# Splitting the first slice of a weight load in two transfers, and the order of the matmuls that read it

## The chip, the core and the metric

The kernel runs on one core of a Trainium2 chip. The metric is the device time of one execution in microseconds (us), given as the median of several executions. Engines are named as in the profile: PE is the matrix engine (PEld its weight loads), DVE the vector engine, ACT the scalar engine, POOL the GpSimd engine, SP the engine that here only issues DMAs.

## What is computed

The program is a retention layer (linear attention with a decay for each head) followed by a two-layer feed-forward block. The reference, cut to what matters:

```python
# q, k, v: (4 batches, 8 heads, 768 steps, 64), float32
gamma = 1.0 - 2.0 ** (-5.0 - np.arange(H)); scale = 1.0 / np.sqrt(D)
for t in range(S):
    state = gamma[None, :, None, None] * state + einsum('bhd,bhe->bhde', k[:, :, t], v[:, :, t])
    y[:, :, t] = scale * einsum('bhd,bhde->bhe', q[:, :, t], state)
x = y.transpose(0, 2, 1, 3).reshape(B * S, H * D)     # 3072 tokens x 512
h = x @ w_in                                          # w_in: 512 x 2048
g = h * np.cos(h)
out = g @ w_out                                       # w_out: 2048 x 512
```

## The kernel before, in words

The order of all work is written out by hand (a manual schedule); each engine runs its own instructions in the order in which the program emits them, and semaphores make an instruction wait for what it reads or overwrites. A small model of time (`Clock`) and a list of PSUM banks (`Banks`, seven banks of 128x512 float32) decide only which bank a unit of work takes next: the one that the model thinks comes free first.

**Retention.** The 768 steps are cut into 6 chunks of 128. A *pair* p (there are 12) is one chunk of two batches. For each pair, q, k and v are loaded (256 KB each; `load`, L130), scaled by the decays and turned to bf16 (`conv_q` L179, `conv_v` L186, `conv_k` L192, on DVE, ACT or POOL), q and k are transposed (by PE in `stage_t`, L214, copied out by DVE at L198; for later pairs by DMA, L224), the 128x128 scores are formed (`stage_a`, L241) and masked by DVE (`stage_m`, L250), and `half_y` (L263 and L268) sums the two terms of y in PSUM, which ACT copies into `xt` (L272). `xt[g]` holds the transposed tokens of a *group* g of two pairs: 4 blocks of 128 model rows (index i, `KIN` = 4) by 512 tokens, of which the first 256 are of the group's first pair and the last 256 of its second. `stage_s` (L285, L290) moves the state on.

**Feed-forward.** An *F unit* is 128 of the 2048 hidden columns for the 512 tokens of one group: four matmuls, one for each i, that sum into one bank (`unit_f`, L316), then cos on ACT (L305) and the product on DVE into `gt` (L309). `pair_f(p, r)` (L327) does the same for one pair's 256 tokens and the four hidden blocks f = 4r to 4r+3, two of them to a bank, so sixteen matmuls of 256 columns into two banks. An *O unit* (`unit_o`, L340) is four matmuls of the second layer; four parts make one block of 128 tokens, copied out by ACT (L347) and stored by SP (L348).

**Weights.** `w_in` is loaded as four slices of 512 hidden columns, one transfer each (`load_w_in`, L135; 512 KB in bf16, read as float32 and cast on the way), `w_out` as four slices of 512 rows (`load_w_out`, L140). F blocks 0 to 3 read slice 0, blocks 4 to 7 slice 1, and so on. All of these are issued by POOL, in one queue with most loads of q, k and v, and with POOL's own conversions between them. The stretch that matters, in POOL's order: v of pair 0, v of pair 1, w_in slices 0 and 1, conversions of v (half of pair 0's first batch at L386, then three whole ones at L186), w_in slice 2, slice 3, w_out slices 0 to 2, k and q of pair 2, w_out slice 3, and v of pair 2, then pair 3.

**The order on PE around the change.** Pairs 0 and 1 go through the retention stages, with filler matmuls (`warm`, L374) between them; then

```python
    half_y(1, 1)
    stage_s(1, nc.scalar.copy)
    pair_f(0, 0)
    pair_f(1, 0)
    for f in range(4, 16):
        unit_f(0, f)
```

so the first four F blocks of group 0 are done pair by pair, and the other twelve as whole units. After them come the O units of group 0 with pair 2's stages between them (`stage_t(2, ...)` after the eighth O unit).

Of the kernel before, what the change touches and what calls it, by code (L numbers as in the profile page):

```python
# [11 lines left out]
BF16 = mybir.dt.bfloat16  # L12
# [35 lines left out]
def kernel(  # L48
# [9 lines left out]
    nc = tc.nc  # L58
# [3 lines left out]
    DM = H * D  # L62
    DF = moe_w_in.shape[1]
    HP = H // 2
    KIN = DM // 128
# [15 lines left out]
    def sb(shape, dt, name):  # L81
        return const.tile(shape, dt, name=name)

    clk = Clock()
    banks = Banks([psum.tile([128, 512], FP32, name=f"bank{i}") for i in range(7)], clk)
# [6 lines left out]
    lnsc = sb([128, 1], FP32, "lnsc")  # L92
    lgv = sb([128, H], FP32, "lgv")

    w_in_sb = [sb([128, KIN, 512], BF16, f"w_in{r}") for r in range(4)]
    w_out_sb = sb([128, KOUT, DM], BF16, "w_out_sb")


# [11 lines left out]
    xt = [sb([128, KIN, 4 * C], BF16, f"xt{i}") for i in range(2)]  # L110
    gt = [sb([128, KOUT, 4 * C], BF16, f"gt{i}") for i in range(2)]
# [13 lines left out]
    def load(eng, p, names):  # L125
        bp, c = divmod(p, NC)
        for n in names:
            t, src = SRC[n[0]]
            b = int(n[1])
            eng.dma_start(  # L130
                out=t[SLOT[p]][b],
                in_=src[2 * bp + b, :, ds(c * C, C)].rearrange("h t d -> t h d"))

    def load_w_in(r):
        nc.gpsimd.dma_start(  # L135
            out=w_in_sb[r],
            in_=moe_w_in[:, ts(r, 512)].rearrange("(i p) f -> p i f", p=128))

    def load_w_out(r):
        nc.gpsimd.dma_start(  # L140
            out=w_out_sb[:, ts(r, 4), :],
            in_=moe_w_out[ts(r, 512), :].rearrange("(p j) m -> p j m", j=4))

    def w_in_t(i, f):
        return w_in_sb[f // 4][:, i].rearrange("p (m j) -> p j m", j=4)[:, f % 4, :]


    load(nc.sync, 0, ("q0", "k0", "q1"))
# [127 lines left out]
    def stage_s(p, copy_st):  # L276
        c = p % NC
        n = p % NB
        if c == NC - 1:
            return  # L280
        for b in range(2):
            for a in range(HP):
                for j in range(2):
                    h = 2 * a + j
                    nc.tensor.matmul(  # L285
                        st_ps[ts(j, 64), b, a, :], lhsT=qk[n][:, b, 1, h, :],
                        rhs=vs[n][:, b, h, :], start=(c == 0 and b == 0 and a == 0),
                        stop=True, skip_group_check=True)
        for j in range(2):
            copy_st(out=stb[(p + 1) % 2][ts(j, 64), :, :, ts(j, 64)], in_=st_ps[ts(j, 64)])  # L290
            clk.run("act" if copy_st == nc.scalar.copy else "dve", 0.65, clk.pe + 0.3)
        clk.run("pe", 0.25)
# [9 lines left out]
    def act(bank, out):  # L302
        cb = cosb[f_no[0] % 3]
        f_no[0] += 1
        nc.scalar.activation(out=cb, in_=bank, func=AF.Sin, bias=halfpi)  # L305
        if len(out.shape) == 3:
            cb = cb.rearrange("p (f t) -> p f t", f=2)
            bank = bank.rearrange("p (f t) -> p f t", f=2)
        nc.vector.tensor_tensor(out=out, in0=bank, in1=cb, op=ALU.mult)  # L309
        clk.run("pe", 0.87)  # L310
        return clk.run("dve", 0.69, clk.run("act", 0.69, clk.pe + 0.1) + 0.1)

    def unit_f(g, f):
        bank = banks.take()
        for i in range(KIN):
            nc.tensor.matmul(bank, lhsT=w_in_t(i, f), rhs=xt[g % 2][:, i, :],  # L316
                             start=(i == 0), stop=(i == KIN - 1))
        banks.give(bank, act(bank, gt[g % 2][:, f, :]))

    def pair_f(p, r, parts=(0, 1)):  # L320

        g, hf = divmod(p, 2)
        for f in [4 * r + 2 * i for i in parts]:
            bank = banks.take()
            for e in range(2):
                for i in range(KIN):
                    nc.tensor.matmul(bank[:, ts(e, 256)], lhsT=w_in_t(i, f + e),  # L327
                                     rhs=xt[g % 2][:, i, ts(hf, 256)],
                                     start=(i == 0 and e == 0), stop=(i == KIN - 1),
                                     skip_group_check=True)  # L330
            banks.give(bank, act(bank, gt[g % 2][:, f : f + 2, ts(hf, 256)]))

    o_bank = {}

    def unit_o(g, j, part):
# [42 lines left out]
    def attend(p):  # L378
        for it in [stage_a(p, b) for b in range(2)]:
            stage_m(p, it)  # L380

    load(nc.gpsimd, 1, ("v0", "v1"))
    load_w_in(0)
    load_w_in(1)
    hh = H // 2
    nc.gpsimd.tensor_tensor(  # L386
        out=vs[0][:, 0, hh:], in0=vf[SLOT[0]][0][:, hh:, :],
        in1=gk[:, 0, hh:].unsqueeze(2).to_broadcast([128, hh, D]), op=ALU.mult)
    conv_v(0, nc.gpsimd, (1,))
    conv_v(1, nc.gpsimd)  # L390
    load_w_in(2)

    warm(8)
# [39 lines left out]
    banks.give(spare, clk.pe)  # L433
    half_y(1, 1)
    stage_s(1, nc.scalar.copy)
    pair_f(0, 0)
    pair_f(1, 0)
    for f in range(4, 16):
        unit_f(0, f)

# [76 lines left out]
    for g in range(2, NG + 1):  # L517
        for s in range(16):
            hf, r = divmod(s, 8)
            p = 2 * (g + 1) + hf  # L520
# [52 lines left out]
```

## Time and profile before

| | |
|---|---|
| median of 6 executions | 210.85 us (209.83 to 211.23) |
| the profiled execution: its time, its span | 211.23 us, 209.4 us |
| granted PE clock | 1.00 |
| busy: PE, DVE, ACT, POOL | 95%, 54%, 55%, 49% of the span |
| w_in: transfers, each, median to landing | 4, 512 KB, 9.0 us |

The span runs from the first to the last instruction of the program; the profiled execution's time is 1.8 us longer. In the views below, times are us from the start of the span, and "L327" is a line of the kernel before. "Busy" of PE counts matmuls that overlap their neighbours, so a full PE row says that PE had no gap, not that it ran at its peak. A DMA's *landing* is the moment when its semaphore tells the waiting engine that all of it has arrived; the trace gives the time from issue to landing for each line, and for a single transfer when the window is narrowed to it.

### The profile page before, as it was taken

What the parts mean: (1) busy time and instruction counts of PE and PEld (TensorE: products, weight loads), DVE (VectorE), ACT (ScalarE), POOL (GpSimd) and SP (SyncE); (2) the same over time, 40 slices, a digit from 0 to 9 for tenths busy, and PEclk for the clock granted to TensorE, in tenths of its full rate; (3) what the DMA queues carried; (4) which work ended last, traced back from release to release, by engine and by line L of the source; (5) the groups of instructions that cost most, each with busy time, mean ns of one, the idle gap of its engine ahead of it and who ended that gap; (6) DMA issues with size and microseconds to landing.
All of it is one profiled execution on the core that took longest, in us unless ns stands there. A gap on an engine that the chain in (4) does not pass through costs nothing.

```text
span 209.4 us, 4170 instructions
## 1 busy us (share of the span) xinstructions
PE 198.7 (95%) x1629; PEld 113.7 (54%) x1652; DVE 114.1 (54%) x188; ACT 114.6 (55%) x193; POOL 102.1 (49%) x118
## 2 busy tenths in 40 slices
PE   7687999999999999999999999999999999999993
PEld 3356554558897555555545455555545444444452
DVE  5691784472967472968874575565565233333000
ACT  6586784057898227477844734744544654553120
POOL 7998325569999999999999500000000000000000
PEclk9999999999999999999999999999999999999999
DMA  6999999969999999988899191181101101110222
GB/s 155 330 239 196 215 243 289 324 172 268 360 231 239 259 262 300 236 263 178 284 128 321 50 103 50 52 105 50 50 3 50 50 0 53 50 52 10 90 72 81
DMA packets 36644, 33.83 MB, mean 162 GB/s; under 512 B 26768, under 2 KB 29072, under 8 KB 36624
## 3 DMA queue, kind: packets, MB, share of 16 engines
q0 software_dynamic: 7808, 20.98, 37.0%
q1 hardware_dynamic: 28672, 12.49, 27.6%
q8 instruction: 13, 0.21, 0.5%
q10 hardware_dynamic: 144, 0.10, 0.1%
q14 instruction: 7, 0.06, 0.1%
HBM read 27.26 MB, written 6.29 MB: 160 GB/s over the span
## 4 chain that ended last, share of the span: by engine, by line
PE 89%; POOL 4%; DMA 4%; issue 1%; DVE 0%; POOLq 0%; DVEq 0%
PE bank L340 38%; PE bank L316 31%; PE bank L327 9%; DMA w_in<-in_moe_w_in_dram 4%; PE bank L241 3%; PE bank L263 2%; PE bank L268 2%; PE bank L357 2%; POOL vf L130 2%; POOL kf L130 1%; PE st_ps L285 1%; PE bank L214 1%; POOL qf L130 1%; DVE ob L362 0%; POOL rel L152 0%
## 5 line engine op out<-in xcount | busy, mean ns | idle before, releaser
L309 DVE TENSOR_TENSOR gt<-bank,cosb 128x512 bf16<-128x512 f32 x96 | 65.4, 690 | 64.4 <-ACT cosb L305 64.1
L305 ACT ACTIVATE cosb<-bank,halfpi 128x512 bf16<-128x512 f32 x96 | 65.6, 688 | 51.5 <-PE bank L316 46.4
L340 PE MATMUL bank<-w_out_sb,gt 128*128 128x512 bf16 x358 | 88.4, 379 | 0.7 <-issue 0.3
L316 PE MATMUL bank<-xt,w_in 128*128 128x512 bf16 x293 | 73.7, 380 | 1.2 <-issue 0.9
L340 PEld LDWEIGHTS <-gt 128*128 128x128 bf16 x368 | 35.5, 98 | 41.2
L316 PEld LDWEIGHTS <-w_in 128*128 128x128 bf16 x304 | 33.5, 114 | 30.1
L250 DVE TENSOR_TENSOR am<-bank,mask 128x512 bf16<-128x512 f32 x48 | 30.4, 681 | 0.8 <-PE bank L241 0.8
L130 POOL DMA_DIRECT2D vf<-in_v_dram x23 | 20.2, 884 | 5.5 <-DMA w_out_sb<-in_moe_w_out_dram 5.5
L347 ACT COPY ob<-bank 128x512 f32<-128x512 f32 x23 | 13.4, 585 | 16.9 <-PE bank L340 16.8
L130 POOL DMA_DIRECT2D kf<-in_k_dram x23 | 20.6, 896 | 3.1 <-DMA w_out_sb<-in_moe_w_out_dram 1.6
L186 POOL TENSOR_TENSOR vs<-vf,gk 128x512 bf16<-128x512 f32 x21 | 21.4, 1040 | 0.2 <-DMA vf<-in_v_dram 0.2
L179 POOL TENSOR_TENSOR qk<-qf,gq 128x512 bf16<-128x512 f32 x18 | 18.5, 1049 | 3.0 <-DMA qf<-in_q_dram 2.3
L327 PE MATMUL bank<-xt,w_in 128*128 128x256 bf16 x160 | 18.4, 273 | 1.6 <-DMA w_in<-in_moe_w_in_dram 1.6
L192 ACT CAST qk<-kf 128x512 bf16<-128x512 f32 x24 | 13.8, 613 | 10.4 <-DMA kf<-in_k_dram 10.4
L327 PEld LDWEIGHTS <-w_in 128*128 128x128 bf16 x160 | 17.2, 114 | 2.0 <-DMA w_in<-in_moe_w_in_dram 1.7
L130 POOL DMA_DIRECT2D qf<-in_q_dram x18 | 16.3, 904 | 1.7 <-DMA w_in<-in_moe_w_in_dram 1.7
L272 ACT CAST xt<-bank 128x512 bf16<-128x512 f32 x24 | 13.0, 587 | 7.3 <-PE bank L268 7.2
L268 PE MATMUL bank<-am,vs 128*64 128x128 bf16 x192 | 11.7, 220 | 0.0
L263 PEld LDWEIGHTS <-stb 128*64 128x64 bf16 x160 | 8.8, 109 | 4.3 <-issue 3.1
L290 DVE CAST stb<-st_ps 64x512 bf16<-64x512 f32 x12 | 8.2, 686 | 4.9 <-PE st_ps L285 4.7
L263 PE MATMUL bank<-qkt,stb 128*64 128x128 bf16 x160 | 10.7, 222 | 0.1
L268 PEld LDWEIGHTS <-vs 128*64 128x64 bf16 x192 | 10.0, 110 | 0.5 <-issue 0.4
(40 smaller groups left out, 77.5 us busy)
## 6 DMA issues: line engine op xcount, KB each, us to landing
kf<-in_k_dram POOLq DMA_DIRECT2D x23, 256.0 KB, 5.5
vf<-in_v_dram POOLq DMA_DIRECT2D x23, 256.0 KB, 5.5
out_dram<-ob SPq DMA_DIRECT2D x23, 256.0 KB, 2.0
qf<-in_q_dram POOLq DMA_DIRECT2D x18, 256.0 KB, 5.4
w_in<-in_moe_w_in_dram POOLq DMA_DIRECT2D x4, 512.0 KB, 9.0
w_out_sb<-in_moe_w_out_dram POOLq DMA_DIRECT2D x4, 512.0 KB, 14.0
qf<-in_q_dram SPq DMA_DIRECT2D x6, 256.0 KB, 8.3
kf<-in_k_dram SPq DMA_DIRECT2D x1, 256.0 KB, 3.4
```

Source lines behind the costliest of these rows:

```text
L130: eng.dma_start(out=t[SLOT[p]][b], in_=src[2 * bp + b, :, ds(c * C, C)].rearrange("h t d -> t h d"))
L179: eng.tensor_tensor(out=qk[p % NB][:, b, 0], in0=qf[SLOT[p]][b], in1=bc(gq, p % NC), op=ALU.mult)
L186: eng.tensor_tensor(out=vs[p % NB][:, b], in0=vf[SLOT[p]][b], in1=bc(gk, p % NC), op=ALU.mult)
L192: nc.scalar.copy(out=qk[p % NB][:, b, 1], in_=kf[SLOT[p]][b])
L250: nc.vector.tensor_tensor(out=am[p % 2][b][j], in0=ap[j], in1=mask.unsqueeze(1).to_broadcast([128, HP, 128]), op=ALU.mult)
L263: nc.tensor.matmul(yp[ts(j, 64), a, :], lhsT=stb[p % 2][:, b, a, ts(j, 64)], rhs=qt(n, b, a), start=True, stop=False, skip_group_check=True)
L268: nc.tensor.matmul(yp[ts(j, 64), a, :], lhsT=vs[n][:, b, 2 * a + j, :], rhs=am[p % 2][b][j][:, a, :], start=(c == 0), stop=True, skip_grou ...
L305: nc.scalar.activation(out=cb, in_=bank, func=AF.Sin, bias=halfpi)
L309: nc.vector.tensor_tensor(out=out, in0=bank, in1=cb, op=ALU.mult)
L316: nc.tensor.matmul(bank, lhsT=w_in_t(i, f), rhs=xt[g % 2][:, i, :], start=(i == 0), stop=(i == KIN - 1))
L327: nc.tensor.matmul(bank[:, ts(e, 256)], lhsT=w_in_t(i, f + e), rhs=xt[g % 2][:, i, ts(hf, 256)], start=(i == 0 and e == 0), stop=(i == KIN ...
L340: nc.tensor.matmul(bank, lhsT=gt[g % 2][:, f, ts(j, 128)], rhs=w_out_sb[:, f, :], start=(f == 0), stop=(f == KOUT - 1))
```

## The change

Slice 0 of w_in is now loaded by two transfers into two tiles: one holds model rows 0 to 255 (i = 0, 1), the other rows 256 to 511 (i = 2, 3). The two stand where the one stood in POOL's order. The first four F blocks are no longer done pair by pair. `first_f` takes four banks, one for each block f of 0 to 3, each holding all 512 tokens. It first runs i = 0 and 1 of the four blocks on the first pair's 256 tokens, then the same on the second pair's 256 tokens (sixteen matmuls of 256 columns in all), and then i = 2 and 3 of each block on all 512 tokens (eight matmuls of 512 columns), each block followed by its cos and product. `gt[0]` is written in whole rows of 512 tokens, as `unit_f` does.

```diff
-    w_in_sb = [sb([128, KIN, 512], BF16, f"w_in{r}") for r in range(4)]
+    w_in_sb = [sb([128, KIN, 512], BF16, f"w_in{r}") for r in range(1, 4)]
+    w_in_0 = [sb([128, KIN // 2, 512], BF16, f"w_in0_{i}") for i in range(2)]
...
     def load_w_in(r):
         nc.gpsimd.dma_start(
-            out=w_in_sb[r],
+            out=w_in_sb[r - 1],
             in_=moe_w_in[:, ts(r, 512)].rearrange("(i p) f -> p i f", p=128))
+
+    def load_w_in_0():
+        for i in range(2):
+            nc.gpsimd.dma_start(
+                out=w_in_0[i],
+                in_=moe_w_in[ts(i, DM // 2), :512].rearrange("(i p) f -> p i f", p=128))
...
     def w_in_t(i, f):
-        return w_in_sb[f // 4][:, i].rearrange("p (m j) -> p j m", j=4)[:, f % 4, :]
+        w = w_in_sb[f // 4 - 1][:, i] if f > 3 else w_in_0[i // 2][:, i % 2]
+        return w.rearrange("p (m j) -> p j m", j=4)[:, f % 4, :]
...
+    def first_f():
+        bank = [banks.take() for _ in range(4)]
+        for hf in range(2):
+            for f in range(4):
+                for i in range(2):
+                    nc.tensor.matmul(bank[f][:, ts(hf, 256)], lhsT=w_in_t(i, f),
+                                     rhs=xt[0][:, i, ts(hf, 256)],
+                                     start=(i == 0 and hf == 0), stop=False,
+                                     skip_group_check=True)
+            clk.run("pe", 0.87)
+        for f in range(4):
+            for i in range(2, KIN):
+                nc.tensor.matmul(bank[f], lhsT=w_in_t(i, f), rhs=xt[0][:, i, :],
+                                 start=False, stop=(i == KIN - 1), skip_group_check=True)
+            clk.run("pe", -0.44)
+            banks.give(bank[f], act(bank[f], gt[0][:, f, :]))
...
     load(nc.gpsimd, 1, ("v0", "v1"))
-    load_w_in(0)
+    load_w_in_0()
     load_w_in(1)
...
     stage_s(1, nc.scalar.copy)
-    pair_f(0, 0)
-    pair_f(1, 0)
+    first_f()
     for f in range(4, 16):
         unit_f(0, f)
```

## The prediction

> **What bounds the kernel now.** I read the chain of work that ended last first, in order of time (start, length, what):
>
> ```profile
> 6.25 3.49 POOL vf L130 x4
> 9.74 8.36 DMA w_in<-in_moe_w_in_dram
> 18.14 3.68 PE bank L327 x32
> 21.87 10.31 PE bank L316 x47
> 32.67 6.42 PE bank L340 x29
> 39.09 0.89 PE bank L214 x16
> 202.46 3.51 PE bank L357 x32
> ```
>
> Up to 18.1 us the end is set by one transfer, slice 0 of w_in, which lands at 9.74 + 8.36 = 18.10. From there to the end the chain is PE without a gap. So a microsecond won for PE near 18 is won at the end, provided that nothing else becomes late. The waits of PE say the same: in the whole span it waits for a DMA once.
>
> ```profile
> PE bank L327 <- DMA w_in<-in_moe_w_in_dram: 1.6, 1, 1.6
> ```
>
> Next the timeline of PE and its weight loads around that place (start, length, engine, line, count; in brackets the idle time before and what ended it):
>
> ```profile
> 15.72 0.27 PE L268 MATMUL bank<-am,vs 128*64 128x128 bf16 x2
> 16.11 0.47 PE L285 MATMUL st_ps<-vs,qk 128*64 128x64 bf16 x16
> 18.13 3.42 PEld L327 LDWEIGHTS <-w_in 128*128 128x128 bf16 x32 [1.67 <-DMA w_in<-in_moe_w_in_dram]
> 18.14 3.68 PE L327 MATMUL bank<-xt,w_in 128*128 128x256 bf16 x32 [1.56 <-DMA w_in<-in_moe_w_in_dram]
> 21.55 10.15 PEld L316 LDWEIGHTS <-w_in 128*128 128x128 bf16 x48
> 21.87 10.31 PE L316 MATMUL bank<-xt,w_in 128*128 128x512 bf16 x47
> ```
>
> PE is through with retention at 16.58. The 32 matmuls of 256 columns take 21.55 - 18.13 = 3.42 us, 0.107 each; those of 512 columns follow each other by (10.31 - 0.38)/46 = 0.216. One of the 48 is missing from the records, so the first most likely began one step before 21.87, at 21.65.
>
> Last, where the next slices land. The view of line L135, narrowed in time until one and then two issues are in it, gives
>
> ```profile
> DMA to landing us min/median/max: 8.4/8.4/8.4
> DMA to landing us min/median/max: 8.4/9.2/10.1
> ```
>
> so slice 1, issued at 10.48, lands at 20.6. Narrowed likewise to the other two, issued at 15.32 and 16.1: 7.8 and 9.6 us, that is 23.1 and 25.7. The four land 2.5, 2.5 and 2.6 us apart although the first two were issued 0.74 apart: the slices are served one after another at about 2.5 us each.
>
> **The change part by part.**
>
> *First half of slice 0.* Half the bytes of a slice served in 2.5 us: it should land 1.25 us ahead of the whole, at 16.85. PE is free at 16.58, and the first pair's `xt` is there: ACT's copies of `xt` run as
>
> ```profile
> 15.22 1.77 ACT L272 CAST xt<-bank 128x512 bf16<-128x512 f32 x3
> ```
>
> of which the first, the last of pair 0, ends near 15.8, and the last two (pair 1) by 16.99. If the matmuls on pair 0 wait for all of `xt`, they start at 17.0 instead. Sixteen matmuls of 256 columns: 1.72 us, to 18.57 (pair 1's eight start at 17.71, after 16.99). The second half lands at 18.1, before it is asked for. Eight matmuls of 512 columns: 1.73, to 20.30 (20.45 with the later start). The same columns run through PE as before, so PE's work is unchanged (16 x 0.107 + 8 x 0.216 = 3.45 against 3.42); it is only started earlier.
>
> *What is late next.* F block 4 needs slice 1, which lands at 20.6. So PE stops again at 20.3 and goes on at 20.63 (after slice 0 the wait ended 0.03 behind the landing). Gain: weight loads 21.55 - 20.63 = 0.92, matmuls 21.65 - 20.64 = 1.01. I take **1.0 us**. This gate makes the term robust: anywhere up to 20.6 - 3.45 = 17.15, a later start of the first half costs nothing. Had slice 1 come before 20.3, the gain would be the whole 1.25 to 1.35.
>
> *One more transfer on POOL's queue.* An issue on L135 (512 rows) takes 0.78 us, on L140 0.56 (fewer, longer rows); a half slice (256 rows) lies between, say 0.66, so two cost 1.32 for 0.78: 0.54 more (0.34 to 0.78). Queued behind it on POOL: slice 1, the conversions of v, slices 2 and 3, w_out, and pair 2's loads. POOL has idle time in the way:
>
> ```profile
> 9.74 1.52 POOL L135 DMA_DIRECT2D w_in<-in_moe_w_in_dram  x2
> 11.56 0.61 POOL L386 TENSOR_TENSOR vs<-vf,gk 128x256 bf16<-128x256 f32 x1 [0.30 <-ACT qk L192]
> 12.33 3.04 POOL L186 TENSOR_TENSOR vs<-vf,gk 128x512 bf16<-128x512 f32 x3 [0.15 <-DMA vf<-in_v_dram]
> 15.32 1.55 POOL L135 DMA_DIRECT2D w_in<-in_moe_w_in_dram  x2
> ```
>
> The 0.30 and 0.15 take 0.45 of the 0.54; v's last conversion ends at 15.46 instead of 15.37 (15.70 at worst). PE reads it at 15.72. And PE's later gate leaves 17.15 - 16.58 = 0.57 of slack. So this costs nothing; without POOL's idle time it would still be inside those 0.57 us. Slice 2 is issued 0.1 later (0.33 at worst) and would be needed at 20.63 + 16 x 0.216 = 24.1, against a landing at 23.1.
>
> *One more transfer on the DMA engines.* Its own cost on the queue (further descriptors, a further completion) no row shows. Lower bound 0: the bytes are the same. Upper bound from the 256 KB loads: they are issued 0.88 apart and land 0.68 to 0.9 apart, data included, so a transfer's own cost cannot be over 0.7. Near neighbours with an equal packet size are the slices at 2.5, which leave nothing to see; I take 0.05 and keep 0 to 0.4 for the range. It delays slice 1 and so comes off the gain one for one.
>
> Here a rule speaks against the change. The Trainium skill's page "DMA: Bandwidth & Descriptors", section "Anatomy of one DMA — SWDGE (gpsimd) path", fits a transfer as some 2.0 us plus its bytes at 436 GB/s, and advises large batches. An estimate by that page, with the 2.0 us paid in line, would put slice 1 at 22.6 and make the kernel 1.0 us slower. The same section puts most of the 2.0 us into the completion, which need not hold up the next transfer.
>
> *Banks, ACT and DVE.* `first_f` holds four of seven banks at once and hands them out late and bunched: block 0 is complete at about 19.0, the fourth at 20.3. A cos takes 0.69, so ACT ends the four at about 22.0 and DVE at 22.7. Blocks 4, 5 and 6 use the other three banks; block 7 starts at 23.2 and block 0's bank is free at 20.6. An F unit takes PE 0.86 and ACT 0.72 with its gap, so the backlog melts. Cost nothing.
>
> *The rest of the span, 1.0 us earlier.* Weights: w_out's slices land (L140, read likewise) at 29.3, 31.7, 34.3 and 39.7, and are asked for at 31.0, 34.5, 38.0 and about 43. Tightest is pair 2: DVE's second conversion ends at 37.94, since q landed late,
>
> ```profile
> 37.25 0.69 DVE L179 TENSOR_TENSOR qk<-qf,gq 128x512 bf16<-128x512 f32 x1 [0.83 <-DMA qf<-in_q_dram]
> 38.92 1.06 PE L214 MATMUL bank<-ident,qk 128*128 128x128 bf16 x16
> ```
>
> and its transposes on PE start about half a microsecond into that group: 39.4 before, 38.4 after. Slack 0.45. ACT's conversion of pair 3's k (bound by its landing) ends at 44.34, where ACT's first copy of an O block would like to start at 44.21: 0.13 late, and PE doesn't wait for that copy. Later transposes by DMA land 2.6 us or more ahead of the scores that read them (pair 6: 75.1 + 5.0 = 80.1 against 82.78).
>
> **Sum.** -1.0 + 0.05 = -0.95. Made against the profiled execution: 211.23 - 0.95 = 210.3. That execution is one of the two slowest of the six; from the median, 210.85 - 0.95 = **209.9 us**. A measurement of this kernel can tell about 0.5%, here 1.05 us, from no change, and the forecast lies just short of that line.
>
> **The rivals.**
>
> *The whole half slice comes through.* If slice 1 lands 0.3 us sooner behind slice 0 than in this execution, the first half is the only gate: gain 1.25 to 1.35, 209.55. For: only 0.3 us are missing. Against: the three spacings of 2.5, 2.5 and 2.6 agree.
>
> *Hidden anyway.* If the halves land within 0.5 us of each other, or all landings come a microsecond earlier in most executions so that PE (free at 16.58) and pair 1's `xt` are the gate, 0 to 0.5 remains: 210.6. For: the six times spread over 1.4 us, and the trace shows one. Against: the slices' regular landings.
>
> *Slower: the transfers share the engines instead of following each other.* Place: the two halves and slice 1, all issued by 11.9 and outstanding together. Counted by its landing, service of slice 0 began at 18.1 - 2.5 = 15.6. Three in equal shares: the halves would both be through after 3 x 1.25 = 3.75 us, at 19.35, slice 1 still at 20.6. PE then starts 1.25 later than before instead of earlier, F block 4 at 19.35 + 3.45 = 22.8: 1.2 slower, 212.05. It decides once the second half lands later than 21.6 - 1.73 = 19.9, or the first later than 18.1. For: no row shows transfers of unequal size in this queue side by side. Against: slices 0 and 1, outstanding together, landed 2.5 apart.
>
> **How the numbers follow.** Forecast 0.68: gain 0.95, its bounds 0.55 (transfer cost 0.4) to 1.25; its centre is near the 1.05 line and a median of a few executions scatters by some 0.3, so I split it 0.36 faster and 0.32 same. Whole half slice 0.10, faster. Hidden 0.10, same. Slower 0.12. Sums: faster 0.46, same 0.42, slower 0.12. The range must leave out no more than 0.2: from 209.3 (the second case with some scatter) to 211.2 (the hidden case with no gain and scatter); what is left out is the slower case and a little at the bottom.
>
> **What would show it.** Right: the first L327-like weight load at about 16.9 with an idle time of 0.3 to 0.5 ended by the first half; no wait ahead of the eight matmuls of 512 columns; a second wait of 0.2 to 0.4 ended by slice 1, which still lands near 20.6; the first L316 weight load near 20.65; O units about 0.95 earlier, and no new PE wait at pair 2. Wrong: the halves landing together, slice 1 landing after 21, an idle PE ahead of pair 2's transposes, or a PE stage after 40 that starts where it did before.

## The result, and the profile after

The changed kernel takes **209.84 us** in the median of 35 executions, against 210.62 of the kernel before in 72. The ratio of the two is 0.9982, with a 95% interval of 0.997 to 0.9995; it is formed from the undisturbed executions of both sides alone, whose means (209.89 and 210.27) lie nearer to each other than the two medians. So the change makes the kernel faster by 0.1 to 0.6 us, less than the 0.5% that a measurement tells from no change. The forecast was 209.9.

The shape of the times says more than the median. Eleven of the 35 lie between 209.50 and 209.53, and none lies under that: the changed kernel has a floor. The kernel before has none there; its fastest execution took 208.92, and seven of the 72 were under 209.4.

The profiled execution took 209.52 us (span 207.7), so it is one of those on the floor. Its weight loads on PE (start, length, engine, line, count; what ended an idle time would stand in brackets) and the landings of the two halves (view of the new load's line, both issues) and of slice 1:

```profile
16.03 0.41 PEld L293 LDWEIGHTS <-qk 128*64 128x64 bf16 x16
16.48 1.67 PEld L346 LDWEIGHTS <-w_in 128*128 128x128 bf16 x16
18.15 1.52 PEld L353 LDWEIGHTS <-w_in 128*128 128x128 bf16 x8
19.77 10.26 PEld L324 LDWEIGHTS <-w_in 128*128 128x128 bf16 x48
```

```profile
L142 POOL DMA_DIRECT2D w_in<-in_moe_w_in_dram x2: 726/732/739, 9.8 to 10.4; - x2
DMA to landing us min/median/max: 5.7/6.1/6.4
```

```profile
L136 POOL DMA_DIRECT2D w_in<-in_moe_w_in_dram x1: 774/774/774, 11.2 to 11.2; - x1
DMA to landing us min/median/max: 8.4/8.4/8.4
```

PE waits for no transfer any more. The halves land at 9.75 + 5.7 = 15.45 and 10.45 + 6.4 = 16.85, slice 1 at 11.17 + 8.4 = 19.57, each ahead of its first use (16.48, 18.15, 19.77). PE goes from the last state update straight into the F blocks, 1.65 us earlier than in the profile before (16.48 against 18.13), and the span is 1.7 us shorter. The chain that ended last no longer holds any DMA:

```profile
7.94 1.20 DVE am L258 x2
10.34 1.20 DVE am L258 x2
11.54 1.19 DVE qkt L206 x2
12.73 1.81 DVE am L258 x3
16.55 1.87 PE bank L346 x16
18.48 1.67 PE bank L353 x7
20.15 9.06 PE bank L324 x42
```

From there to the end nothing else has moved. The time of an execution less the start of its first F weight load is 193.10 for the kernel before (211.23 - 18.13), 193.04 for the changed one, and within 0.1 of that in every profile below in which nothing waits between the first and the last F block. So an execution's time can be read as the moment when PE enters the F blocks (where nothing waits after it): by 193.05, 209.5 is 16.45, the median before (210.62) is 17.57, and its fastest (208.92) is 15.87.

What holds PE until 16.45 in the changed kernel? These are POOL and PE around the first state update (L293):

```profile
11.17 0.77 POOL L136 DMA_DIRECT2D w_in<-in_moe_w_in_dram  x1
11.94 0.65 POOL L411 TENSOR_TENSOR vs<-vf,gk 128x256 bf16<-128x256 f32 x1
12.52 3.05 POOL L194 TENSOR_TENSOR vs<-vf,gk 128x512 bf16<-128x512 f32 x3
15.50 1.55 POOL L136 DMA_DIRECT2D w_in<-in_moe_w_in_dram  x2
```

```profile
13.20 0.23 PEld L293 LDWEIGHTS <-qk 128*64 128x64 bf16 x9
13.64 0.20 PEld L293 LDWEIGHTS <-qk 128*64 128x64 bf16 x7 [0.20 <-issue]
```

POOL has no idle time in these rows; before, it had 0.30 and 0.15. The sixteen loads of the state update, eight for each batch, break off after nine: the other batch's v is the first of the three conversions at L194, and it ends at 12.52 + 1.06 = 13.58. The loads go on 0.06 behind that. The view calls this pause "issue", and the chain passes POOL by; that it is a wait for POOL is at this point a reading of times, which the experiments test.

### The profile page after: what moved, and what is told of

Read it like the earlier page. It is cut to its first block, busy times and chain, and to the rows that moved or that the text cites. A ratio compares the mean times of both kernels' runs of the same rounds, so it can differ in the third digit from the quotient of the medians.

```text
span 207.7 us, 4155 instructions
## 1 busy us (share of the span) xinstructions
PE 198.8 (96%) x1621; PEld 113.0 (54%) x1644; DVE 113.5 (55%) x188; ACT 114.4 (55%) x193; POOL 102.7 (49%) x119
## 4 chain that ended last, share of the span: by engine, by line
PE 93%; DVE 4%; issue 1%; ACT 0%; DVEq 0%
PE bank L365 38%; PE bank L324 32%; PE bank L335 7%; PE bank L271 3%; PE bank L249 3%; PE bank L276 2%; PE bank L399 2%; DVE am L258 2%; PE bank L382 2%; PE bank L222 1%; PE st_ps L293 1%; DVE qkt L206 1%; PE bank L346 1%; PE bank L353 1%; DVE qk L187 1%
## 5 line engine op out<-in xcount | busy, mean ns | idle before, releaser
L324 PEld LDWEIGHTS <-w_in 128*128 128x128 bf16 x304 | 33.5, 114 | 30.3
L131 POOL DMA_DIRECT2D kf<-in_k_dram x23 | 20.6, 898 | 2.4 <-DMA w_out_sb<-in_moe_w_out_dram 1.5
L194 POOL TENSOR_TENSOR vs<-vf,gk 128x512 bf16<-128x512 f32 x21 | 21.4, 1042 | 0.0
L335 PE MATMUL bank<-xt,w_in 128*128 128x256 bf16 x128 | 14.7, 273 | 0.0
L335 PEld LDWEIGHTS <-w_in 128*128 128x128 bf16 x128 | 13.8, 113 | 0.4
```

The lines of the kernel that those rows point to most:

```text
L131: eng.dma_start(out=t[SLOT[p]][b], in_=src[2 * bp + b, :, ds(c * C, C)].rearrange("h t d -> t h d"))
L194: eng.tensor_tensor(out=vs[p % NB][:, b], in0=vf[SLOT[p]][b], in1=bc(gk, p % NC), op=ALU.mult)
```

## The experiments

**Theory A**: POOL's queue makes the floor. Two half issues cost 0.73 each where the one cost 0.78, so the conversions of v come 0.68 later wherever POOL does not wait for v itself, and when the slices land early PE waits for them. The change gains when slice 0 lands late and loses when it lands early. **Theory B**: the extra issue is hidden, and the gain is small because slice 0 mostly lands early; PE's and DVE's own chain makes the floor. All comparisons are with the kernel before on the same chip.

**1. The split alone.** The changed kernel with the old order:

```diff
-    first_f()
+    pair_f(0, 0)
+    pair_f(1, 0)
```

> The split alone: slice 0 in two transfers, but the first four F blocks still done pair by pair, so the first bank already needs both halves. Theory A (POOL's queue: the second issue of slice 0 is paid by the conversions of v behind it and by PE after them, whenever the slices land early): nothing is gained from the first half, and the fastest executions rise from about 208.9 (before) to about 209.5 (the changed kernel's floor); median of about 210.6 to 210.9, none under 209.4; PE's matmuls of the first state update wait for POOL's conversion of v. Theory B (landings: the extra issue costs nothing, the gain is small because the slices mostly land early): the same as before, median 210.6, with executions under 209.3 as before.

Measured: median 210.28 (12 executions, 209.61 to 210.94) against 210.41; ratio 1.0002 (0.9982 to 1.0022). No execution came under 209.6, where the kernel before, beside it, had seven of 35 under 209.6 down to 209.11. So the fast end is missing, as A expects and B does not; but with seven in 35, twelve executions without one would come by luck in 7% of cases, so this run alone does not decide. The median is 0.3 below the 210.6 to 210.9 that A gave, and the interval is too wide to say more. In the profile the sixteen loads of the first state update take 0.48 us, against 0.33 where nothing holds them (experiment 5), a mild form of the pause that A expects. The profile also shows where the old order has to stop (PE):

```profile
16.47 0.41 PE L335 MATMUL bank<-xt,w_in 128*128 128x256 bf16 x2
17.45 1.72 PE L335 MATMUL bank<-xt,w_in 128*128 128x256 bf16 x14 [0.57 <-DMA w_in<-in_moe_w_in_dram]
```

Two matmuls run on the first half (landed at 16.15), then PE waits until the second lands, 1.25 us later. The new order has sixteen matmuls for the first half, enough for this gap.

**2. The order alone.** Slice 0 again in one transfer, read by `first_f`:

```diff
-    w_in_0 = [sb([128, KIN // 2, 512], BF16, f"w_in0_{i}") for i in range(2)]
+    w_in_0 = sb([128, KIN, 512], BF16, "w_in0")
...
+        nc.gpsimd.dma_start(
+            out=w_in_0, in_=moe_w_in[:, :512].rearrange("(i p) f -> p i f", p=128))
```

> The order alone: slice 0 in one transfer, read by the new order of matmuls. Both theories: the first matmul waits for the whole slice as before, so the same as before within 0.2 us, median 210.6, fastest about 208.9. If instead the order itself costs or gains (four banks held at once, late and bunched products), it differs from before by more than 0.3.

Measured: median 210.57 against 210.41, lowest 209.15; ratio 0.9996 (0.997 to 1.0022). The order by itself costs and gains nothing that can be seen. One execution of twelve lies under 209.5, which none of the changed kernel's does by more than 0.03; that the fast end is back rests on this one. In the profile slice 0 landed at 9.74 + 6.9 = 16.65, a microsecond and a half before its landing in the profile before, and PE did not wait for it.

**3. Without the second half's transfer.** Only the first half is loaded, and the matmuls of rows 256 to 511 read it in place of the second. The kernel leaves out a part of the weights, so its output is not the layer's; PE does the same work:

```diff
-        for i in range(2):
+        for i in range(1):
...
-        w = ... else w_in_0[i // 2][:, i % 2]
+        w = ... else w_in_0[0][:, i % 2]
```

> The changed kernel with the second half of slice 0 never loaded: the matmuls of model rows 256 to 511 of the first four F blocks read the first half's tile in its place. PE, ACT and DVE do the same work; POOL has one issue fewer, and 256 KB less are moved, so slice 1 lands about 1.25 us sooner. Theory A: the floor falls from 209.5 by the price of the issue to about 208.9, and nearly all executions lie there. Theory B: PE was not waiting in the fast executions of the changed kernel, so the floor stays at 209.5 and only the slower executions move there.

Measured: median 209.56 against 210.41, lowest 209.04; ratio 0.9969 (0.9947 to 0.999). Three of twelve are under the floor of the changed kernel, so the floor has fallen, against B. (256 KB less are moved as well, so this run does not tell the issue from the bytes; 4 and 12 do.) But A was wrong that nearly all would lie near 208.9: five of the twelve stay between 209.50 and 209.64. The profile (209.53) shows what took POOL's place:

```profile
11.46 0.61 POOL L411 TENSOR_TENSOR vs<-vf,gk 128x256 bf16<-128x256 f32 x1 [0.23 <-DMA vf<-in_v_dram]
12.46 3.04 POOL L194 TENSOR_TENSOR vs<-vf,gk 128x512 bf16<-128x512 f32 x3 [0.40 <-DMA vf<-in_v_dram]
```

POOL has time now, and waits 0.23 and 0.40 us for v to land; its conversions start at 12.46, where they started at 12.52. So in this execution the landing of v is a next bound right under the issue.

**4. More POOL work in the same place.** A repeat of the half conversion, into a buffer that is overwritten unread:

```diff
     hh = H // 2
+    nc.gpsimd.tensor_tensor(out=vs[2][:, 0, hh:], in0=vf[SLOT[0]][0][:, hh:, :], ...)
```

> The changed kernel with one more POOL instruction between the issues of w_in and the conversions of v: a repeat of the half conversion (128x256, 0.65 us) into a buffer that nobody reads before it is overwritten. Theory A: POOL's queue is the floor, so it rises by 0.5 to 0.65, from 209.5 to about 210.1, median about 210.2. Theory B: PE has 0.57 us of slack behind POOL, so the time moves by no more than 0.1.

Measured: median 210.10 against 210.41, ratio 1.0 (0.998 to 1.0019). Six of twelve executions took exactly 210.06: the floor is there again, 0.56 above the old one. POOL and PE's loads in its profile:

```profile
12.51 0.64 POOL L414 TENSOR_TENSOR vs<-vf,gk 128x256 bf16<-128x256 f32 x1
13.08 3.04 POOL L194 TENSOR_TENSOR vs<-vf,gk 128x512 bf16<-128x512 f32 x3
```

```profile
13.76 0.23 PEld L293 LDWEIGHTS <-qk 128*64 128x64 bf16 x9
14.19 0.20 PEld L293 LDWEIGHTS <-qk 128*64 128x64 bf16 x7 [0.20 <-issue]
...
17.04 1.68 PEld L346 LDWEIGHTS <-w_in 128*128 128x128 bf16 x16
18.71 1.52 PEld L353 LDWEIGHTS <-w_in 128*128 128x128 bf16 x8
20.62 0.36 PEld L324 LDWEIGHTS <-w_in 128*128 128x128 bf16 x3 [0.39 <-DMA w_in<-in_moe_w_in_dram]
```

POOL's conversions start 13.08 - 12.52 = 0.56 later, the loads break off after nine again and go on 0.55 later, the F blocks start 17.04 - 16.48 = 0.56 later, and the floor lies 0.56 higher. What POOL does longer ahead of these conversions is paid in full at the end, so PE has no slack behind them in an execution on the floor, against the 0.1 at most that B gave. That settles the floor for A. The last row shows the gate that the prediction named, slice 1 at 20.6, in a weight load's wait of 0.39; PE was still busy then and lost less than 0.1 by it (210.17 for this execution, less 193.05 and 17.04).

**5 to 7. Less POOL work.** In 5, ACT converts six heads of the first batch instead of four (`hh`); in 7, seven; in 6, six, and slice 1 is issued behind the second conversion, the edit's second half, which 5 and 7 do not have:

```diff
-    hh = H // 2
+    hh = 6
...
     load_w_in_0()
-    load_w_in(1)
...
     conv_v(0, nc.gpsimd, (1,))
+    load_w_in(1)
```

> The changed kernel with less POOL work in front of the conversions: of the first batch of v, ACT converts six of eight heads instead of four, POOL two instead of four (128x128 instead of 128x256, an estimated 0.43 us instead of 0.65 from the 0.65 and 1.04 us of the two larger sizes). Theory A (POOL's queue is the floor): the floor falls by about 0.2, to 209.3; median about 209.6. Theory B (the floor is PE's or DVE's own chain): floor 209.5, or a little above since ACT works 0.53 us longer ahead of the first state update.

> The same, and slice 1 of w_in issued behind the second conversion of v instead of ahead of it, which takes its 0.77 us from in front of the first state update and leaves the end of the last conversion where it was; slice 1 is then issued at about 12.8 instead of 11.2. Theory A: the first state update no longer waits for POOL; the floor falls by 0.2 to 0.4 against the changed kernel, to 209.1 to 209.3, if slice 1 still lands by 19.6; if the later issue leaves the DMA engines without work, slice 1 lands after 20 and the median rises above 210. Theory B: 209.5 or more.

> The changed kernel with seven heads on ACT and one on POOL (128x64, an estimated 0.33 us instead of 0.65); ACT's four conversions become seven, 0.8 us more, so that the first half of y waits for ACT at about 12.8. Theory A: POOL's floor falls by 0.3, but ACT takes its place: 209.3 to 209.6. Theory B: above 209.5.

Measured, against 210.40: 209.73 (lowest 209.31, ratio 0.9981, 0.996 to 1.0001); 209.91 (lowest 209.31, ratio 0.9988, 0.9966 to 1.001); 209.98 (lowest 209.51, ratio 0.9993, 0.9975 to 1.0012). POOL's whole conversions start at 12.32, 11.56 and 12.21 instead of 12.52. In 5 and 6 one execution of twelve each took 209.31, 0.2 under the old floor, as A gave it; in 7 none did, and none of the three medians separates from the others. In the profile of 5 the loads of the state update no longer break off, and PE still entered the F blocks at 16.48. There the bound lies at the start of the kernel, and it is PE itself (5 first, then 6):

```profile
5.01 1.48 PE L399 MATMUL bank<-gt 128*128 128x512 bf16 x3
6.29 0.63 PE L222 MATMUL bank<-ident,qk 128*128 128x128 bf16 x4
```

```profile
4.75 0.81 PE L399 MATMUL bank<-gt 128*128 128x512 bf16 x3
5.85 0.40 PE L222 MATMUL bank<-ident,qk 128*128 128x128 bf16 x4 [0.29 <-ACT qk L200]
```

In 5 the filler matmuls and the first transposes run at little more than half the pace of those in 6, so DVE starts to copy the transposes out at 6.96 instead of 6.28; from there to the state update it is 6.54 us in 5 and 6.57 in 6. The profiles of 7 and 8 show 6.96 too, and a PE that is ready at the same time as in 5. So an execution near 209.5 can have this bound in place of POOL's, in experiment 3 too. In the changed kernel's profile DVE started at 6.65, 0.31 ahead of 5, and PE entered the F blocks at the same 16.48; an estimate from these rows is that POOL cost that execution 0.3 us. What sets PE's pace at the start was not tested.

Number 6 shows two other limits side by side (PE):

```profile
15.48 0.25 PE L276 MATMUL bank<-am,vs 128*64 128x128 bf16 x2 [0.22 <-POOL vs L194]
...
20.18 1.05 PE L324 MATMUL bank<-xt,w_in 128*128 128x512 bf16 x4 [0.27 <-DMA w_in<-in_moe_w_in_dram]
```

The last conversion of v holds PE for 0.22, and slice 1, issued 1.4 us later than in the changed kernel, lands at 12.55 + 7.6 = 20.15 and holds it for 0.27 by this row. By the times it cost 0.54: PE entered the F blocks at 16.25, which by 193.05 gives 209.30, and the execution took 209.84. What an earlier start of PE wins, the later issue gives back.

**8. The kernel before, a second profile.** No edit.

> The kernel before, once more, for a second profile. Theory A: slice 0 lands at another time than 18.1, PE's first F matmul moves with it, and the span is about 209.4 less that shift, down to the point where PE is ready (16.5 or earlier). Theory B expects the same reading of the wait, but with PE ready never before 16.4 and so no span under 207.6.

```profile
11.28 0.63 POOL L386 TENSOR_TENSOR vs<-vf,gk 128x256 bf16<-128x256 f32 x1
11.85 3.04 POOL L186 TENSOR_TENSOR vs<-vf,gk 128x512 bf16<-128x512 f32 x3
```

```profile
16.03 0.41 PEld L285 LDWEIGHTS <-qk 128*64 128x64 bf16 x16
18.38 3.42 PEld L327 LDWEIGHTS <-w_in 128*128 128x128 bf16 x32 [1.94 <-DMA w_in<-in_moe_w_in_dram]
```

One execution, 211.44 us: slice 0 landed at 18.35, later still than the 18.10 of the first profile. Here v landed early enough that POOL had no idle time, and its conversions started at 11.85, 0.67 ahead of the changed kernel's 12.52: the whole price of the second issue, with no idle time to hide it. It did not catch the kernel before in one of its short executions, so that side of A rests on the times alone.

**9 and 10. A load moved from POOL to SP.** k of pair 0's second batch, in the changed kernel and in the one before:

```diff
-    load(nc.sync, 0, ("q0", "k0", "q1"))
-    load(nc.gpsimd, 0, ("k1",))
+    load(nc.sync, 0, ("q0", "k0", "k1", "q1"))
```

> The changed kernel with one load (k of pair 0, second batch) issued by SP, third of four, instead of first by POOL: POOL's whole queue starts 1.0 us sooner, and q of the second batch is issued 0.5 later by SP. Theory A (POOL's queue is the changed kernel's floor): the floor of 209.5 vanishes, executions down to about 208.9 appear, median 209.3 to 209.6, limited then by the landing of v, by the first q and k, or by slice 1. Theory B: floor and median stay at 209.5 and 209.8.

> The same move in the kernel before. Both theories: POOL is not what bounds the kernel before, slice 0 is, and its landing is set by the DMA engines and not by its issue: median within 0.3 of 210.5. If the earlier issue brings slice 0 in earlier, up to 1 us faster, and then the change itself is worth less beside it.

Both expectations failed. Medians 217.77 and 241.16 against 210.10; ratios 1.0076 (1.0039 to 1.0112) and 1.0149 (1.0071 to 1.0228), which go by the five shortest of twelve executions and the two shortest of six, from a wide scatter (211.1 to 250.9 and 212.0 to 255.9). In the profile of 9 (211.89 us) q, now last of four on SP, lands late, DVE waits for it and PE for DVE (here DVE, then PE):

```profile
9.22 0.69 DVE L186 TENSOR_TENSOR qk<-qf,gq 128x512 bf16<-128x512 f32 x1 [2.20 <-DMA qf<-in_q_dram]
```

```profile
9.96 0.62 PE L221 MATMUL bank<-ident,qk 128*128 128x128 bf16 x8 [2.49 <-DVE qk L186]
```

That explains about 2 of the 2.4 us by which PE enters the F blocks later (18.92), and makes both runs useless for the question of POOL. It does not explain the far longer executions: in the profile of 10 (255.86 us) PE waits 36.9 us in all for the transposes by DMA. Why a load moved at the start should slow transposes 50 us later was not found.

**11. The changed kernel again**, beside 9 and 10.

> The changed kernel again, beside the two others on the same chip: median 209.8, a third of its executions within 0.03 of 209.5, none under it.

Measured: 209.94 (209.47 to 210.36) against 210.10; ratio 0.9993 (0.9968 to 1.0019). The kernel before went down to 208.84 beside it. The floor held but for 0.03. The interval tells this gain neither from none nor from the 0.4 us of the ratio above. In the profile (209.97) nothing waits for w_in and the state update does not break off; PE enters the F blocks at 16.92 because k of pair 0 landed late (ACT waited 1.46 us for it). So above the floor the times spread for reasons other than slice 0.

**12. POOL relieved without moving a load to another queue.** The first issue goes behind the two index ramps that POOL writes at the start:

```diff
-    load(nc.gpsimd, 0, ("k1",))
     nc.gpsimd.iota(pos, ...)
     nc.gpsimd.iota(rel, ...)
+    load(nc.gpsimd, 0, ("k1",))
     load(nc.gpsimd, 1, ("q0", "q1", "k0", "k1"))
```

> The changed kernel with POOL's first load issue (k of pair 0, second batch) moved behind the two index ramps that POOL writes at the start, instead of ahead of them. In the profile of the changed kernel POOL sits idle for 0.8 us ahead of that issue, so the ramps fit there, and everything behind the issue on POOL comes 0.3 us sooner (2.40 instead of 2.69 for the next load, as in the run with that load on SP). Theory A (POOL's queue is the floor): floor 209.2 instead of 209.5, median about 209.6 to 209.7. Theory B: floor unchanged at 209.5.

```profile
0.84 0.15 POOL L157 IOTA pos<- 128x6 f32 x1 [0.39 <-POOLq L581]
0.95 0.24 POOL L159 IOTA rel<- 128x128 f32 x1
1.38 1.05 POOL L131 DMA_DIRECT2D kf<-in_k_dram  x1 [0.19 <-issue]
2.42 1.76 POOL L131 DMA_DIRECT2D qf<-in_q_dram  x2
...
12.16 3.07 POOL L194 TENSOR_TENSOR vs<-vf,gk 128x512 bf16<-128x512 f32 x3
```

Measured: median **209.51** (10 executions, 209.19 to 210.03) against 210.62; ratio 0.9956 (0.9936 to 0.9975). The ramps now run in time in which POOL was idle, the conversions of v start 12.52 - 12.16 = 0.36 earlier, and the fastest execution lies 0.31 under the floor of the changed kernel, as A expected to within 0.01. Five of the ten lie under 209.47, the lowest of the changed kernel's 47. The median came out a little under the 209.6 to 209.7 that A gave. The interval against the kernel before lies clear of one; the 0.9 us is still less than the 0.5% named above. Side by side with the changed kernel (209.84 and 209.94) it was not timed.

## Why the prediction was right, and where it was wrong

*The first half lands 1.25 us ahead of the whole, and transfers follow one another.* Right: 1.4 us apart in the changed kernel's profile, 1.2 to 1.5 in six others, though 2.1 and 2.0 in experiments 5 and 6. With that the slower rival falls (shares of the engines would have landed both together), and so does the estimate in which the 2.0 us of the Trainium skill's page "DMA: Bandwidth & Descriptors" (section "Anatomy of one DMA — SWDGE (gpsimd) path") are paid in line for each transfer: in most profiles less than that lay between the two landings, data included. Slice 1 landed 2.7 (changed kernel) and 2.5 us (experiment 1) behind the second half, against 2.5 before, so a further transfer's own cost is 0 to 0.2 there; in experiments 4 and 12 it was 3.7 and 3.3 behind, which stays unexplained.

*The order costs nothing, and the rest of the span follows.* Right: experiment 2, and the constant 193.05 between the first F load and the time of the execution.

*The size of the wait.* Mis-sized: the profiled execution before had slice 0 landing at 18.10, and the gain of 1.0 us was read from it. A second profile of the same kernel has 18.35; in eight profiles of kernels that differ from it only behind that issue or by the split, all of slice 0 has landed at 16.65 to 17.6. The median of 210.62 stands for an entry into the F blocks at 17.57. The prediction saw the spread of 1.4 us in the times, and the "hidden anyway" rival named it, but the sum did not use it: moving to the median shifted the start of the scale and left the gain as large as for the latest landings. Of the signs that the prediction gave for being right, the missing wait ahead of the matmuls of 512 columns is there, but neither of its two waits: PE waits for neither half nor for slice 1, its first F load is at 16.48 and not 16.9, and F block 4's at 19.77 and not 20.65. The gain of 0.4 us lies in the 0 to 0.5 of the "hidden anyway" rival.

*The next gate.* Named as slice 1 at 20.6. In the changed kernel's profile that gate is not reached (19.57 against 19.77). It is close, though: slice 1 holds the loads for 0.39, 0.31 and 0.18 in experiments 4, 5 and 7, at less than 0.1 at the end each time, and in experiment 6, where it was issued later, PE itself for 0.27.

*POOL's extra issue costs nothing.* This step failed, and it failed in its cover, not in its price (0.68 measured, 0.54 said). The cover was taken as POOL's 0.45 of idle time and PE's slack of 0.57 behind the last conversion, both read from an execution with late landings; the second profile of the kernel before has no such idle time. The first reader was overlooked: in the changed kernel's profile the state update of pair 0 would have gone on at 13.43 but for the second conversion, which ended at 13.58, 2 us before the last one. And slack against a gate that varies is no slack when the gate opens early. The cost is the floor of 209.50, some 0.6 above the fastest executions before (0.3 in the profiled one, by the estimate above); experiment 4 shows that POOL is what it is made of, and experiment 12 that it falls when POOL starts earlier.

So, read across executions since no single one shows both kernels, the change takes a microsecond or more from those with a late slice 0 (from an entry at 18.1 or 18.4 to one at 16.5 or a little later) and adds up to 0.6 to those with an early one; for the fast side no profile of the kernel before exists. The forecast of 209.9 hit the median of 209.84 with some luck, by a gain that was counted too high from a base that stood too high; the ratio gives 0.4 us, not 0.95.

## What to carry to other kernels

A wait for a transfer, read from one profile, has the size of that execution's landing: where the times of a kernel spread by more than the gain in question, read the sum at the early and at the late end too. A transfer that is split in two pays a second issue on its queue, and when it arrives early enough, what is computed behind it on that engine can become the next bound; look for the first reader of each of those results, not only the last. Before adding an issue, look for idle time earlier on the same queue that can be filled by moving work into it (experiment 12).

## What the runs showed of the hardware

- An issue on POOL hardly gets cheaper with fewer rows: 256 rows of 2 KB took 0.73 us, 512 rows 0.77. Two halves of a transfer cost nearly two issues.
- The same transfer, issued at the same time (9.74 to 9.75), landed at 16.65 in one execution (experiment 2) and at 18.10 and 18.35 in others (the kernel before).
- POOL's first DMA issue began at 1.26 us with POOL idle for 0.82 before it, and at 1.38 with two small ramps run from 0.84 on (experiment 12).
- Three filler matmuls of PE early in the kernel took 1.48 us in one execution (experiment 5, at 5.01) and 0.81 in another (experiment 6, at 4.75).
- Four loads in a row on SP instead of three, with one taken off POOL, went with executions up to 255.9 us long (experiments 9 and 10), and in the one profiled, PE waited for transposes by DMA; the cause stays open.
